# A planned tie between GpSimd and VectorE at their shared port

## The chip, the cores and the metric
The kernel runs on one core of one Trainium2 chip. The metric is the time of one execution in device microseconds; the kernel before takes 1047.97 us as the median of three runs (1047.88, 1047.97 and 1050.83 us). Five engines work side by side, each with its own queue: TensorE (PE), ScalarE (ACT), VectorE (DVE), GpSimd (POOL) and SyncE (SP), which issues the DMAs.

## The reference
Attention with a cut-off is followed by two feed-forward layers on all 2304 tokens:

```
scores = (q @ k.T) / 8                      # batch 4, 8 heads, 576 x 576, head size 64
thresh = max(scores) - tau                  # per row, tau = 0.02
scores = where(scores >= thresh, scores, -1e9)
attn   = exp(scores - max) / (sum + 1e-9)
x      = (attn @ v), heads side by side     # 2304 x 512
h = x @ w_in;   x = (h * clip(h + 3, 0, 6) / 6) @ w_out          # 512 -> 2048 -> 512
h = x @ w2_in;  out = (h / (1 + exp(-1.702 h))) @ w2_out         # 512 -> 2048 -> 512
```

## The kernel before, in words
Products are made at more than half precision by splitting each operand into a high part and a low part (the rest after rounding): three matmuls (high x high, high x low, low x high) stand for one. The high part is written by a ScalarE copy or a VectorE cast; the low part is a subtraction, by VectorE or GpSimd (`tt`, L523, which all such element-wise operations of two tensors share). The split parts of activations are `xh`/`xl` and `g`/`gl`, of keys and queries `kqv`, of weights `inhring`/`inlring` and `outhring`/`outlring`. Weights arrive as 64-bit numbers and are decoded into floats by a chain on ScalarE, VectorE (L575, L576, L577) and GpSimd (`wmstg<-wmstg,wrstg`).

In the first 400 us attention runs head pair by head pair: TensorE makes a 128x576 tile of scores, VectorE takes the row maximum (L837), ScalarE the exponential (L840), VectorE masks and sums (L841), GpSimd or ScalarE multiplies by the reciprocal sum (L856, L864). Half of the first layer is worked in between (L1061, L1086), on 256 or 320 tokens at a time. Then come the second half of the first layer, from 400 to 650 us, and the second layer (L1295, L1431), which uses seven products where eight would be plain, with extra sums and differences `c`, `u`, `p` on VectorE and GpSimd.

Nothing of the order is left to a scheduler. A class `Plan` collects every operation with its engine, an assumed cost and what it reads and writes. `order` plays the plan through as a list schedule: each engine takes its ready operation with the smallest rank (the ranks are stored in the file), and writes a planned start for each operation to `self.start`. For the operations named in `PORT` it keeps VectorE and GpSimd apart: one of them isn't started while one of the other engine runs, by the planned times.

```
PORT = {DVE: {"W", "WH", "WD", "XHB", ...}, POOL: {"kl", "qs", "ql", "vl", "W", "WD", "GD", "N", ...}}
if port[o] and taken[DVE + POOL - e] > t:
    est[o] = taken[DVE + POOL - e]
```

`settle` sorts all operations by planned start, and `fill` turns them into a list of functions that are called in this order, with some matmuls on constants (L1622) put into planned gaps of TensorE. On the chip each engine works off its own operations in this order, and waits for another engine only where a tile's data or its buffer demand it. The planned times themselves are not enforced. `LAT` holds assumed latencies from one engine to another; from VectorE to GpSimd it is 155 ns. The names of operations in the plan (`W` weights, `GL` low part of a gated activation, `XL` low part of an input, `N` normalisation, `RM` spread of reciprocals, `GT` gate on VectorE) are what `PORT` refers to.

Of the kernel before, what the change touches and what calls it, by code (L numbers as in the profile page):

```python
# [3 lines left out]

# [17 lines left out]
PE, ACT, DVE, POOL, SP, DMA = range(6)  # L22

LAT = {
    (PE, PE): 0, (PE, ACT): 197, (PE, DVE): 197, (ACT, PE): 200, (ACT, ACT): 200, (ACT, DVE): 150, (ACT, POOL): 170,
    (DVE, PE): 200, (DVE, ACT): 120, (DVE, DVE): 127, (DVE, POOL): 155, (POOL, PE): 203, (POOL, ACT): 200, (POOL, DVE): 220, (POOL, POOL): 130,
    (SP, DMA): 53, (ACT, DMA): 53, (DMA, PE): 943, (DMA, ACT): 943, (DMA, DVE): 943, (DMA, POOL): 1000, (DMA, SP): 943,
}
# [148 lines left out]
class Plan:  # L177
# [189 lines left out]

    def fill(self, order, make):

        used = [[] for _ in range(BANKS)]  # L370
        for b in self.banks:
            ops = [x[0] for x in b.access]
            used[b.bank].append((min(self.start[o.n] for o in ops), max(self.start[o.n] + o.cost for o in ops) + 250))
        out, end = [], 0.0
        for op in order:
            if op.eng == PE:
                t, s = end, self.start[op.n]
                end = max(end, s + op.cost)
                count = int((s - t) / 450 if s < 12000 else (s - t - 300) / 216)
                if count > 0:  # L380
                    slack = max((min([t - y for _, y in u if y <= t] + [1e9]), -i) for i, u in enumerate(used) if not any(x < s and y > t for x, y in u)) if any(not any(x < s and y > t for x, y in u) for u in used) else None
                    if slack is not None:
                        out.append(make(-slack[1], count))
            out.append(op.fn)
        return out


# [1 line left out]
def tile_top_attention_moe_moe2(  # L389
# [64 lines left out]
    pl = Plan()  # L454
    changed = []

    def add(eng, cost, time, name, fn, rd=(), wr=(), touch=(), alt=None):
        op = pl.add(eng, cost, time, fn, rd, wr, name, touch)
        op.alt = alt
        for c, names in changed:  # L460
            if any(b.pool in names for b in op.bufs):
                op.deps.add(c)
        return op

    def move(time, name, nbytes, fn, rd=(), wr=(), eng=SP):

        op = add(eng, 590, time, name, fn, rd, wr)
        add(DMA, nbytes / 360 * PACE.get(name, 1.0), time, name, lambda: None, rd, wr).deps.add(op)
# [24 lines left out]
    def mark():  # L493
        return Buf(pl, "mark", 1 << 30, None, "")
# [169 lines left out]
    def keep(kept, time):  # L664

        def put(n, reg, src, lo, size):
            d, m = kept.setdefault(n, (dram.tile([P, DM], F32, name="kept"), mark()))
            move(time, "KS", 4 * P * size, lambda: nc.sync.dma_start(out=d[:, reg * HALF:reg * HALF + size], in_=src.t[:, lo:lo + size]), [src], [(m, reg)])

        return put  # L670
# [930 lines left out]
    for q in range(2):  # L1601
        for c0, n in [x for y in ([BLOCKS[1:2], BLOCKS[:1], BLOCKS[2:]], [BLOCKS[1:], BLOCKS[:1]])[q] for x in y]:
            moe2(c0, n, w, t, q == 0, q == 1)
            if left:
                i, kind = left.pop(0)
# [8 lines left out]

    add(ACT, 1500, t, "TL", lambda: nc.scalar.activation(out=gate_b.t, in_=half_b.t, func=ACTF.Gelu_apprx_sigmoid), [half_b], [gate_b]).deps |= {o for o in pl.ops if o.name == "X"}

    def busy(i, count):

        def run():
            t = pools["pm"].tile([P, 512], F32, tag=f"pm{i}", name="pm")  # L1620
            for _ in range(count):
                nc.tensor.matmul(t[:, :P], two_b.t, two_b.t, start=True, stop=True)  # L1622

        return run

    order = pl.settle()
    with tc.manual_schedule():
        for fn in pl.fill(order, busy):
            fn()
# [51 lines left out]
```

## Time and profile before

| | |
|---|---|
| median of 3 runs | 1047.97 us (1047.88 to 1050.83) |
| profiled execution | 1051.93 us, span 1050.1 us |
| TensorE clock, granted share | 0.997 |
| busy: TensorE, VectorE, ScalarE, GpSimd | 98%, 79%, 64%, 55% of the span |

The span runs from the first to the last instruction; the profiled execution's own time holds also what lies around it. A row of a group of instructions gives line, engine, operation, what it writes and reads, shape and count, then busy time and mean duration, then the engine's idle time ahead of them and who ended it. In a timeline an entry in brackets is the idle time of the engine ahead of the instruction, and what ended it.

### The profile page before, as it was taken

To read this page: it belongs to the slowest core of one execution; us is meant where nothing else is said; L and a number is where in the kernel's file an instruction comes from. 1 tells how busy PE (TensorE), PEld (TensorE's weight loads), DVE (VectorE), ACT (ScalarE), POOL (GpSimd) and SP (SyncE) were. 2 spreads that over 40 slices of the span, in tenths; PEclk is the share of its full clock that TensorE was granted. 3 is DMA by queue.
4 is the path that set the end of the run, shared out by engine and by line. 5 is a ranking of instruction groups with operands and counts; after the bars stand their busy time and mean duration, and the time that the engine had idled before them with its cause. 6 is when DMAs were issued, how large, how long until landed. Compare 5 with 4: busy or idle time off the path is not lost. (4 is left out here: it accounts for less than half of the span.)

```text
span 1050.1 us, 21245 instructions
## 1 busy us (share of the span) xinstructions
PE 1028.7 (98%) x7560; PEld 956.4 (91%) x7560; DVE 828.6 (79%) x1700; ACT 667.0 (64%) x1395; POOL 577.0 (55%) x681
## 2 busy tenths in 40 slices
PE   8999999999999999999999999999999999999998
PEld 6787887798979898999899999999999999999998
DVE  7999999998999885768877687756787998656644
ACT  5988678776766665665344444576757766655553
POOL 5577866675656552665564435445654435546452
PEclk9999999999999999999999999999999999999999
DMA  7434466676877665445645768827464896443412
GB/s 237 119 123 125 132 180 181 177 221 165 236 221 190 192 195 150 143 134 179 199 127 178 246 218 268 310 97 255 140 209 156 269 296 193 155 161 104 140 49 72
DMA packets 113194, 187.46 MB, mean 179 GB/s; under 512 B 10816, under 2 KB 62656, under 8 KB 111040
## 3 DMA queue, kind: packets, MB, share of 16 engines
q1 hardware_dynamic: 112944, 185.80, 57.4%
q8 instruction: 60, 0.98, 0.4%
q14 instruction: 46, 0.38, 0.1%
q10 hardware_dynamic: 144, 0.29, 0.1%
HBM read 117.77 MB, written 68.29 MB: 177 GB/s over the span
## 5 line engine op out<-in xcount | busy, mean ns | idle before, releaser
L837 DVE TENSOR_REDUCE nm<-ps 128x1 f32<-128x576 f32 x144 | 105.9, 749 | 14.3 <-PE ps L781 10.5
L523 POOL TENSOR_TENSOR g<-t,g 128x256 fp32r<-128x256 f32 (+2 forms) x84 | 76.1, 909 | 68.9 <-ACT g L520 53.3
L840 ACT ACTIVATE e<-ps,nm 128x576 f32<-128x576 f32 x128 | 93.0, 738 | 31.7 <-DVE nm L837 28.9
L1086 PE MATMUL pm<-g,outhring 128*128 128x256 f32 (+1 forms) x512 | 106.2, 299 | 0.7 <-DVE g L523 0.5
L841 DVE SCALAR_TENSOR_TENSOR e<-ps,th,e 128x576 f32<-128x576 f32 x128 | 102.0, 810 | 6.1 <-ACT e L840 3.0
L1086 PE MATMUL py<-g,outhring 128*128 128x432 f32 (+2 forms) x384 | 99.6, 344 | 2.7 <-DVE yc L523 2.1
L520 ACT ACTIVATE g<-t 128x256 fp32r<-128x256 f32 (+3 forms) x177 | 86.0, 489 | 24.7 <-DVE t L1073 11.3
L523 POOL TENSOR_TENSOR wmstg<-wmstg,wrstg 128x512 uint32<-128x512 uint32 x40 | 55.5, 1390 | 82.2 <-DVE wmstg L577 39.7
L1061 PE MATMUL pm<-xh,inhring 128*128 128x256 f32 (+1 forms) x320 | 97.8, 306 | 0.9 <-DVE t L1073 0.7
L1061 PE MATMUL pm<-xh,inlring 128*128 128x256 f32 (+1 forms) x320 | 94.6, 296 | 0.0
L1061 PE MATMUL pm<-xl,inhring 128*128 128x256 f32 (+1 forms) x320 | 94.5, 295 | 0.0
L781 PE MATMUL ps<-kqv 128*128 128x288 f32 x480 | 82.2, 303 | 3.2 <-DVE e L841 1.9
L1086 PEld LDWEIGHTS pm<-g,outhring 128*128 128x128 f32 x512 | 82.1, 189 | 1.9 <-DVE g L523 0.8
L781 PEld LDWEIGHTS ps<-kqv 128*128 128x128 f32 x480 | 68.1, 190 | 11.0 <-issue 4.5
L1086 PE MATMUL pm<-g,outlring 128*128 128x256 f32 (+1 forms) x256 | 75.7, 296 | 0.0
L1086 PEld LDWEIGHTS py<-g,outhring 128*128 128x128 f32 x384 | 69.9, 191 | 6.2 <-DVE yc L523 2.5
L1086 PE MATMUL py<-g,outlring 128*128 128x432 f32 (+2 forms) x192 | 65.5, 341 | 0.0
L1061 PEld LDWEIGHTS pm<-xh,inhring 128*128 128x128 f32 x320 | 60.6, 189 | 2.5 <-DVE t L1073 0.9
L523 DVE TENSOR_TENSOR g<-t,g 128x256 fp32r<-128x256 f32 (+2 forms) x76 | 49.3, 650 | 16.3 <-ACT g L520 16.0
L1061 PEld LDWEIGHTS pm<-xl,inhring 128*128 128x128 f32 x320 | 60.6, 189 | 0.0
L523 POOL TENSOR_TENSOR kqv<-qk,kqv 64x576 fp32r<-64x576 f32 (+1 forms) x39 | 56.3, 1443 | 7.6 <-DVE kqv L757 3.2
L1061 PEld LDWEIGHTS pm<-xh,inlring 128*128 128x128 f32 x320 | 60.4, 189 | 0.0
(265 smaller groups left out, 3655.2 us busy)
## 6 DMA issues: line engine op xcount, KB each, us to landing
turned<-tr SPq DMA_DIRECT2D x16, 1024.0 KB, 4.1
et<-turned SPq DMA_DIRECT2D x64, 256.0 KB, 5.9
wrawstg<-in_w1i_dram SPq DMA_DIRECT2D x16, 512.0 KB, 3.9
wrawstg<-in_w1o_dram SPq DMA_DIRECT2D x16, 512.0 KB, 3.7
wrawstg<-in_w2i_dram SPq DMA_DIRECT2D x16, 512.0 KB, 4.2
wrawstg<-in_w2o_dram SPq DMA_DIRECT2D x16, 512.0 KB, 4.1
qk<-in_k_dram SPq DMA_DIRECT2D x24, 288.0 KB, 3.9
qk<-in_q_dram SPq DMA_DIRECT2D x24, 288.0 KB, 4.1
```

Of the source, the lines that this page charges most:

```text
L520: return lambda: nc.scalar.activation(out=o(), in_=i(), func=ACTF.Copy, **kw)
L523: return lambda: (nc.vector if eng == DVE else nc.gpsimd).tensor_tensor(out=o(), in0=a(), in1=b(), op=op)
L781: nc.tensor.matmul(ps.t[:, i, :SH], q, w[hd].t[:, i * SH:(i + 1) * SH], start=a, stop=z)
L837: add(DVE, 672, K("R", s), "R", lambda: nc.vector.tensor_reduce(out=nm.t[:, c], in_=ps.t[:, :, :SH], op=ALU.max, axis=AX.XY, negate=True), ...
L840: add(ACT, 624, K("X", s), "X", lambda: nc.scalar.activation(out=ev(), in_=ps.t[:, :, :SH], func=ACTF.Exp, bias=nm.t[:, c]), [ps, (nm, s)] ...
L841: add(DVE, 736, K("M", s), "M", lambda: nc.vector.scalar_tensor_tensor(out=ev(), in0=ps.t[:, :, :SH], scalar=th.t[:, c], in1=ev(), op0=ALU ...
L1061: nc.tensor.matmul(ph.t[:, :n], a, v, start=(cc == 0 and i == 0), stop=(cc == KC - 1 and i == 2))
L1086: nc.tensor.matmul(py.t[:, :n], a, v, start=(st and i == 0), stop=(sp and i == 2))
```

## The change
While the functions are listed, `fill` now keeps what each VectorE operation's function returns, the instruction, under the operation's number. For each GpSimd operation named in `PORT` it looks for the latest VectorE operation (named in `PORT` or not) whose planned end plus 155 ns is no later than the planned start of the GpSimd operation, half a nanosecond allowed, and adds a synchronising dependency of the one's instruction on the other's. If a function returned nothing, the next earlier VectorE operation is taken, and a GpSimd operation whose own function returns nothing gets no dependency. The order of the functions stays.

```diff
     def fill(self, order, make):
+        made, dve = {}, [o for o in order if o.eng == DVE]
+        ends = [self.start[o.n] + o.cost + LAT[DVE, POOL] for o in dve]
+
+        def keep(op):
+            return lambda: made.__setitem__(op.n, op.fn())
+
+        def behind(op, i):
+            return lambda: self.tie(op.fn(), next((made[o.n] for o in dve[i::-1] if made[o.n] is not None), None))
...
-            out.append(op.fn)
+            i = bisect_right(ends, self.start[op.n] + 0.5) - 1 if op.eng == POOL and self.port[op.n] else -1
+            out.append(keep(op) if op.eng == DVE else behind(op, i) if i >= 0 else op.fn)
         return out
...
+    def tie(ins, first):
+        if ins is not None and first is not None:
+            tc.add_manual_dep(ins.ins, first.ins.name, mybir.DependencyInfo(mybir.DependencyClass.Sync, mybir.DependencyReason.ANTI), reason="port")
+
+    pl.tie = tie
```

## Rows read from the trace of the kernel before

**Rows 1.** The page's first part: busy us, share of the span, instructions.

```profile
PE 1028.7 (98%) x7560; PEld 956.4 (91%) x7560; DVE 828.6 (79%) x1700; ACT 667.0 (64%) x1395; POOL 577.0 (55%) x681
```

**Rows 2.** Busy us of each engine (and instructions) in five stretches of the span.

```profile
0.00:200.00 200.00, 191.26 (x1364) 157.00 (x1364) 184.59 (x446) 154.76 (x301) 136.37 (x200) 1.00 0.55 160
200.00:400.00 200.00, 198.36 (x1524) 176.34 (x1525) 180.89 (x432) 138.00 (x289) 120.36 (x194) 1.00 0.71 199
400.00:650.00 250.00, 246.51 (x1504) 235.80 (x1503) 187.63 (x339) 126.99 (x238) 124.73 (x102) 0.99 0.59 182
650.00:1000.00 350.00, 347.17 (x2794) 342.06 (x2793) 255.25 (x451) 223.42 (x509) 176.55 (x168) 1.00 0.57 192
1000.00:1050.10 50.10, 45.42 (x381) 45.22 (x379) 20.24 (x36) 23.86 (x60) 19.00 (x18) 0.98 0.17 53
```

**Rows 3.** Waits of TensorE by releaser: us in total, times, longest us.

```profile
PE py L1086 <- DVE yc L523: 2.1, 2, 1.5
...
PE pm L907 <- DVE pk L856: 0.2, 1, 0.2
```

**Rows 4.** VectorE's instructions by shape: busy us, mean ns, idle before and its releasers.

```profile
L523 DVE TENSOR_TENSOR gl<-c,g 128x512 fp32r<-128x512 f32 x39 | 31.8, 818 | 8.8 <-ACT g L520 4.0 <-ACT t L1374 2.3 <-PE pm L1431 1.3
...
L523 DVE TENSOR_TENSOR g<-t,g 128x256 fp32r<-128x256 f32 x41 | 22.1, 539 | 11.6 <-ACT g L520 11.5
...
L523 DVE TENSOR_TENSOR yc<-py,yc 128x512 f32<-128x512 f32 x28 | 19.1, 686 | 5.2 <-PE py L1431 3.4 <-POOL yc L523 1.5
...
L523 DVE TENSOR_TENSOR c<-pm,p 128x256 f32<-128x256 f32 x40 | 16.8, 419 | 11.5 <-ACT p L520 4.7 <-PE pm L1295 3.9 <-ACT g L520 2.5
...
L523 DVE TENSOR_TENSOR c<-c,p 128x256 f32<-128x256 f32 x15 | 12.3, 821 | 0.4 <-POOL u L523 0.3
```

**Rows 5.** Timeline of all engines, 498 to 510 us: start, us, instruction, idle before.

```profile
498.28 0.69 DVE L577 SCALAR_TENSOR_TENSOR wmstg<-wrawstg,wmstg 128x512 uint32<-128x512 uint32 x1
...
499.11 1.35 POOL L523 TENSOR_TENSOR wmstg<-wmstg,wrstg 128x512 uint32<-128x512 uint32 x1 [1.83 <-DVE wmstg L577]
...
501.43 0.49 DVE L1073 SCALAR_TENSOR_TENSOR t<-t,pm 128x320 f32<-128x320 f32 x1
...
502.03 1.47 POOL L523 TENSOR_TENSOR inlring<-wsstg,inhring 128x512 fp32r<-128x512 f32 x1
...
502.45 1.40 DVE L523 TENSOR_TENSOR g<-t,g 128x320 fp32r<-128x320 f32 x1
...
503.44 1.55 POOL L523 TENSOR_TENSOR inlring<-wmstg,inhring 128x512 fp32r<-128x512 f32 x1
...
503.78 1.50 DVE L523 TENSOR_TENSOR wmstg<-wmstg,wsstg 128x256 f32<-128x256 f32 x1
...
506.07 0.56 PE L1086 MATMUL py<-g,outhring 128*128 128x320 f32 x2 [0.52 <-DVE yc L523]
...
508.76 0.80 PE L1086 MATMUL py<-g,outhring 128*128 128x256 f32 x2 [1.55 <-DVE yc L523]
```

**Rows 6.** Timeline of all engines, 80 to 87 us.

```profile
81.13 1.46 POOL L523 TENSOR_TENSOR outlring<-wmstg,outhring 128x512 fp32r<-128x512 f32 x1
81.37 1.36 DVE L1074 CAST g<-t 128x256 fp32r<-128x256 f32 x1
...
86.23 0.97 PE L821 MATMUL ps<-kqv 128*128 128x288 f32 x3 [0.87 <-PE pm L983]
```

**Rows 7.** Timeline of all engines, 486 to 492 us.

```profile
487.47 0.29 PE L1061 MATMUL pm<-xh,inlring 128*128 128x256 f32 x1
...
487.59 0.28 PE L1061 MATMUL pm<-xh,inhring 128*128 128x256 f32 x1
...
489.79 1.29 POOL L523 TENSOR_TENSOR wmstg<-wmstg,wrstg 128x512 uint32<-128x512 uint32 x1 [3.95 <-DVE wmstg L577]
489.91 1.45 DVE L523 TENSOR_TENSOR g<-t,g 128x256 fp32r<-128x256 f32 x1 [0.26 <-ACT g L520]
...
491.42 0.38 PE L1086 MATMUL py<-g,outhring 128*128 128x256 f32 x1 [0.62 <-DVE g L523]
```

More of the change, by code (lines that the diff above doesn't have):

```diff
@@ L1 @@
 from base64 import b85decode
+from bisect import bisect_right
 from contextlib import ExitStack
```

## Prediction, made before the result
> **What bounds the kernel now.** I read the engines' shares first [rows 1]. TensorE is busy for 1028.7 us of a span of 1050.1 us, so at most 21.4 us can go without touching its matmuls. VectorE is at 79% and GpSimd at 55%. The reader is to see that the target is not an engine's work but TensorE's idle time, and that GpSimd has 473 us in which it could wait.
>
> Then the same by stage [rows 2]. TensorE idles 8.7 us in the first 200 us, 1.6, 3.5 and 2.8 us in the three stages that follow, and 4.7 us in the last 50 us, where the last matmul is over and results drain. In the first 400 us VectorE is busy for 365 us of 400: there a microsecond that VectorE loses reaches TensorE soon. After 400 us it has a quarter to a third of its time free, and a lost microsecond matters only where TensorE is already waiting.
>
> Then TensorE's waits by releaser [rows 3]. Without the first matmul's wait for a constant, 17 rows name VectorE, from "py <- yc" at 2.1 us to "pm <- pk" at 0.2 us, 23 waits and 11.9 us in all. None names GpSimd. So GpSimd does not hold TensorE up directly; if it does harm, it does so through VectorE.
>
> That it does is seen in the mean of one VectorE operation by shape [rows 4]. A 128x256 subtraction or addition with one input in PSUM takes 419 ns. The same operation with both inputs in SBUF has a mean of 821 ns (c<-c,p) and 539 ns (g<-t,g). At 128x512 it is 686 ns with PSUM and 818 ns (gl<-c,g) without. These three shapes alone lose (821-419)x15 + (539-419)x41 + (818-686)x39 = 6.0 + 4.9 + 5.1 = 16 us; other shapes whose operands are all in SBUF are stretched in the same way, the ones with PSUM are not.
>
> The timeline shows how [rows 5]. At 502.03 us GpSimd starts a subtraction of 1.47 us. At 502.45 VectorE starts g<-t,g (128x320) and is done only at 503.85, after GpSimd; the same work behind a free port takes 0.49 us (VectorE's t<-t,pm of that size in [rows 5]). At 503.44 GpSimd has started its next subtraction, and VectorE's operation at 503.78, a 128x256 addition that takes 0.42 us behind a free port [rows 4], takes 1.50 us. VectorE is now (1.40 - 0.49) + (1.50 - 0.42) = 2.0 us late, and TensorE idles 0.52 us at 506.07 and 1.55 us at 508.76, both times for VectorE's yc. A port that one engine holds for its whole operation delays the other, one for one, and the delay arrives at TensorE.
>
> **The change part by part.** It adds to each GpSimd operation named in PORT, except the RM multiplications (their function returns nothing, so nothing can be tied), one wait on a VectorE operation. From 681 GpSimd instructions [rows 1] go 46 memsets, one addition for the second identity and the 20 RM operations: about 614 ties. It removes and reorders nothing, and adds no work to VectorE, ScalarE, TensorE or SP.
>
> The partner is the last VectorE operation, whatever its kind, whose planned end plus 155 ns is not after the planned start. I took the partners from the planned starts that the kernel before computes. Where the plan was kept, the partner is long done, and the wait costs nothing but its issue. Where GpSimd runs ahead of the plan, it now stands back until VectorE has caught up.
>
> The gain, case by case. Both GpSimd operations of [rows 5] run ahead. The partner of the one at 502.03 is the very g<-t,g that it blocks, and that of the one at 503.44 lies five operations behind the one that it blocks. With the ties both VectorE operations keep their short time, VectorE is 2.0 us earlier, and the 2.07 us of idle time go. In [rows 6] the GpSimd operation at 81.13 is tied to a t<-t,pm three operations behind the cast at 81.37, which takes 1.36 us, as it cannot end before GpSimd; TensorE's wait at 86.23 (0.87 us, named after its own matmul, because VectorE's late reduction and masking free the PSUM tile at the last moment) goes. Five more cases have this shape, with GpSimd operations at 19.20, 109.39, 175.88, 707.31 and 852.40 us and TensorE idle for 0.37, 0.92, 0.54, 0.53 and 0.35 us behind them. Sum: 2.07 + 0.87 + 2.71 = 5.65 us in eight waits.
>
> Two corrections. The end of a matmul is modelled: in [rows 7] one takes 0.29 us while the next starts 0.12 us after it, so each idle stretch is shown about 0.17 us too short; eight of them make 1.4 us, sum 7.0 us. And idle below the threshold of the view, and waits of VectorE's own followers on ScalarE, are not in the list; as VectorE's stretch in the three shapes above is 16 us and the cases above recover some 8 us of stretch in all, I add 3 us, an estimate bounded below by 0 and above by the other 6.3 us of the 11.9 us that VectorE releases. Sum: 10 us.
>
> The cost. A GpSimd operation that has to wait starts some 0.14 us after the VectorE operation's end: 498.28 + 0.69 = 498.97, and GpSimd starts at 499.11 [rows 5]. If all 614 waited, that were 86 us of GpSimd's 473 us of idle time; if none waits it is zero, and a wait that is already met adds at most an instruction of the sequencer. I take zero for the end of the kernel, because no row of [rows 3] has TensorE waiting for GpSimd. The cover is that slack, stage by stage: 63.6 us in the first 200 us, over 170 us from 650 to 1000 [rows 2].
>
> What is queued behind a waiting operation: GpSimd's own next ones, in order. The subtraction at 503.44 would stand back some 3 us, until its partner has run, and the g<-t,g of GpSimd behind it starts about 1 us later. Its result feeds the second product of an output group that comes three gates later, several microseconds on; the decoded weights are used over 100 us later. The buffers that these operations free are taken by ScalarE's next decode, which is not near TensorE either. SP's queue sees later stores only through GpSimd's few results that are stored.
>
> What is late next: where the partner lies ahead of the VectorE operation that is blocked, and is already done, nothing is protected. That is so for GpSimd at 489.79 us [rows 7], whose partner was done, while VectorE's g<-t,g waits for ScalarE until 489.91 and is then blocked (TensorE idle 0.62 us). Such cases stay. By the partners I expect about half of VectorE's stretch to stay.
>
> A rule of the Trainium skill weighs against the change. In [rows 4] c<-pm,p has its 419 ns although GpSimd is busy in more than half the time. SBUF — State Buffer, "Who interferes with whom", says that a VectorE instruction with at most one SBUF input, outside the two-port modes, does not contend with GpSimd, and the row agrees. By it a tie to a reduction or masking that reads PSUM protects no port and only holds GpSimd up; what that could cost is the third rival. By the cases above the sum stays a gain of 10 us.
>
> **The sum.** The profiled execution took 1051.93 us; less 10 us it is 1041.9. That execution lies 3.96 us above the median of the three runs, 1047.97 us, like the slowest of the three. For the median I take off the same 10 us: 1038 us.
>
> **The rivals.** First, more is gained: all 23 waits that VectorE ends go, 11.9 + 23 x 0.17 = 15.8 us, and some of the idle below the threshold, 2 us: 1030 us. For it: in the first 400 us VectorE is nearly full, and there a late start carries over from one head to the next. Against it: half the collisions are not covered.
>
> Second, nothing comes of it: GpSimd, held to the plan on one side only, collides with the next VectorE operation in place of this one; a VectorE operation that waits for ScalarE finds the port taken, as in [rows 7]. The exchange leaves VectorE's stretch where it is: 1047 to 1049 us. That the ties don't work at all (an operation's function that returns nothing) would look the same; only for RM does the code show it.
>
> Third, slower: in the first 200 us GpSimd becomes the bound. There it has 63.6 us free, and about 160 tied operations among its 200. A VectorE operation takes 184.59/446 = 0.41 us there; if each tie costs half of one and the 0.14 us, that is 160 x 0.35 = 56 us, and GpSimd is nearly full. It then delivers kl, ql and the scaled rows late, TensorE's scores wait for it, and a tenth of the 56 us that reaches TensorE makes 5.6 us: 1054 us. It decides once less than some 10 us of GpSimd's idle time are left in this stage. For it: the ties do not ask what the partner reads. Against it: most partners are done when GpSimd starts.
>
> **How the numbers follow.** The forecast has a chance of 0.50, more gain 0.26, nothing 0.14, slower 0.10. The forecast's own range is 1033 to 1044 us, by 4 us for what is not recovered and 5 us for what is not listed. Two in ten are left out at 1027 below and 1048 above. A run of this kernel can be told from no change at 0.3%, 3.1 us, so faster is below 1044.8 us: 0.50 + 0.26 and a little of the second case, 0.78; same 0.12; slower 0.10.
>
> **What would show it.** Right: the three shapes of [rows 4] fall towards 419 and 686 ns while c<-pm,p stays; VectorE's busy time falls by 20 us or more at the same count; the stretched pairs of [rows 5, 6] are gone, with GpSimd starting behind its partner; GpSimd's waits on VectorE grow by tens of microseconds; TensorE's waits on yc, gl and e shrink. Wrong: TensorE waiting for GpSimd's results (kqv, g, xl), GpSimd over 90% in the first 200 us, or VectorE's means unchanged. If VectorE's busy time falls and the end does not move, the lost time was hidden, and the step from VectorE to TensorE is the one that failed.

## Result and profile after

The changed kernel takes 1037.29 us (median; 1035.86 to 1037.47), the kernel before, timed beside it, 1048.48 us (1047.88 to 1050.83). The ratio is 0.9886, 95% interval 0.9868 to 0.9904: 11 to 12 us faster. The forecast was 1038 us, a gain of 10 us. The profiled execution took 1037.47 us, span 1035.7 us; the one before took 1051.93 us, which is 3.5 us above the median of its runs, so the two profiles lie 14.5 us apart and hold some 3 us more than the medians do. Line L523 and those up to the end of the products' code stand 11 lines lower (L534 for L523), the matmuls on constants 17 (L1639 for L1622).

The page's first part (busy us, share, instructions), which answers to [rows 1]:

```profile
PE 1023.2 (99%) x7560; PEld 954.6 (92%) x7560; DVE 792.7 (77%) x1700; ACT 667.2 (64%) x1395; POOL 566.0 (55%) x681
```

At the same counts VectorE's busy time fell by 35.9 us and GpSimd's by 11.0 us. ScalarE's is as before (667.2 against 667.0 us). Busy time by stage, which answers to [rows 2]; the columns are the stretch, its length, then TensorE, weight loads, VectorE, ScalarE and GpSimd, and the granted clock:

```profile
0.00:200.00 200.00, 194.38 (x1390) 159.87 (x1392) 183.89 (x458) 158.08 (x307) 136.11 (x204) 1.00 0.57 164
200.00:400.00 200.00, 199.38 (x1542) 177.26 (x1539) 178.12 (x421) 135.97 (x285) 117.07 (x191) 1.00 0.71 197
400.00:650.00 250.00, 248.86 (x1513) 239.60 (x1510) 181.12 (x347) 130.48 (x244) 129.18 (x107) 1.00 0.62 190
650.00:1000.00 350.00, 349.31 (x2864) 346.79 (x2863) 235.12 (x453) 226.82 (x518) 170.57 (x169) 1.00 0.56 188
```

TensorE's idle time is now 5.6, 0.6, 1.1 and 0.7 us in these stages (8.7, 1.6, 3.5 and 2.8 us in [rows 2]). With the last stretch it is 12.5 us against 21.4. That is 8.9 of the 14.4 us by which the two spans differ; the other 5.5 us are in TensorE's busy time, at the same counts. GpSimd is as busy in the first 200 us as it was, 68%.

TensorE's waits by releaser (us in total, times, longest), which answers to [rows 3]:

```profile
PE pm L1639 <- DVE two L552: 1.4, 1, 1.4
PE py L1097 <- POOL g L534: 1.0, 1, 1.0
PE ps L792 <- DVE e L852: 0.9, 3, 0.3
...
PE ps L792 <- DVE rc L859: 0.2, 1, 0.2
```

Without the wait for the constant `two`, VectorE now releases 10 waits and 3.8 us, against 23 and 11.9. All waits for `yc`, `gl`, `c` and `p` are gone. The second row is new: TensorE waits for GpSimd.

VectorE by shape (busy us, mean ns), which answers to [rows 4]:

```profile
L534 DVE TENSOR_TENSOR gl<-c,g 128x512 fp32r<-128x512 f32 x39 | 28.3, 729 | 8.8 <-ACT g L531 3.7 <-ACT t L1385 2.5 <-PE pm L1442 1.3
...
L534 DVE TENSOR_TENSOR yc<-py,yc 128x512 f32<-128x512 f32 x28 | 19.2, 688 | 8.5 <-PE py L1442 5.5 <-POOL yc L534 1.5 <-ACT outhring L531 1.2
...
L534 DVE TENSOR_TENSOR g<-t,g 128x256 fp32r<-128x256 f32 x41 | 18.9, 461 | 11.4 <-ACT g L531 11.1
...
L534 DVE TENSOR_TENSOR c<-pm,p 128x256 f32<-128x256 f32 x40 | 16.8, 421 | 13.2 <-PE pm L1306 5.8 <-ACT p L531 4.7 <-ACT g L531 2.5
...
L534 DVE TENSOR_TENSOR c<-c,p 128x256 f32<-128x256 f32 x15 | 8.7, 577 | 0.4 <-POOL u L534 0.3
```

The three shapes with both inputs in SBUF fell (818 to 729, 539 to 461, 821 to 577 ns); the two with an input in PSUM stay at 688 and 421 ns.

The stretch of [rows 5] begins here at 494.7 us. Timeline of VectorE (start, us, instruction):

```profile
494.68 0.48 DVE L534 TENSOR_TENSOR g<-t,g 128x320 fp32r<-128x320 f32 x1
495.08 0.42 DVE L534 TENSOR_TENSOR wmstg<-wmstg,wsstg 128x256 f32<-128x256 f32 x1
...
497.10 1.11 DVE L534 TENSOR_TENSOR xl<-xr,xh 128x432 fp32r<-128x432 f32 x2
```

and of GpSimd, with the idle time ahead and its releaser in brackets:

```profile
495.24 1.41 POOL L534 TENSOR_TENSOR inlring<-wsstg,inhring 128x512 fp32r<-128x512 f32 x1 [0.77 <-DVE g L534]
497.84 1.52 POOL L534 TENSOR_TENSOR inlring<-wmstg,inhring 128x512 fp32r<-128x512 f32 x1 [1.20 <-DVE xl L534]
```

g<-t,g takes 0.48 us (1.40 before) and the addition 0.42 us (1.50 before). The first GpSimd subtraction waits for g<-t,g, the second for the low part `xl`, 2.3 us after the addition that it used to block. The cast of [rows 6] takes 0.29 us (1.36 before), and TensorE has no idle time between 80 and 87 us:

```profile
80.38 0.29 DVE L1085 CAST g<-t 128x256 fp32r<-128x256 f32 x1
```

The case of [rows 7] has gone too. VectorE's g<-t,g came 0.12 us behind GpSimd's decode step before; now it comes 0.03 us ahead of it and takes 0.42 us (timeline of all engines, 482 to 485 us):

```profile
483.40 0.42 DVE L534 TENSOR_TENSOR g<-t,g 128x256 fp32r<-128x256 f32 x1
483.43 1.55 POOL L534 TENSOR_TENSOR wmstg<-wmstg,wrstg 128x512 uint32<-128x512 uint32 x1 [3.31 <-ACT g L531]
```

TensorE's 0.62 us at this place are gone. With nine ties only (run one below) the collision is still there and TensorE waits 0.9 us.

What is left and what is new. GpSimd's next decode step blocked VectorE's L575 before (timeline, 495.9 to 497 us):

```profile
496.00 1.28 POOL L523 TENSOR_TENSOR wmstg<-wmstg,wrstg 128x512 uint32<-128x512 uint32 x1 [0.63 <-DVE wmstg L577]
496.18 1.39 DVE L575 TENSOR_SCALAR wmstg<-wmstg 128x512 f32<-128x512 f32 x1
```

In the change the same GpSimd operation blocks the operation after that one (timeline of all engines, 488 to 493 us):

```profile
488.79 1.40 POOL L534 TENSOR_TENSOR wmstg<-wmstg,wrstg 128x512 uint32<-128x512 uint32 x1 [0.35 <-DVE yc L534]
...
489.07 1.39 DVE L587 TENSOR_SCALAR wmstg<-wmstg 128x512 uint32<-128x512 uint32 x1
```

GpSimd waits for its partner `yc`, and the next VectorE operation at the port, a decode step with a mean of 470 ns, takes 1.39 us. This collision has stayed and only moved by one operation; TensorE has no idle time near it. And the new wait (timeline of all engines, 512 to 518 us):

```profile
513.64 1.30 POOL L534 TENSOR_TENSOR wmstg<-wmstg,wrstg 128x512 uint32<-128x512 uint32 x1 [1.88 <-DVE t L1199]
...
513.96 1.26 DVE L586 TENSOR_SCALAR wmstg<-wmstg 128x512 f32<-128x512 f32 x1 [0.41 <-ACT wmstg L585]
...
515.14 0.48 DVE L534 TENSOR_TENSOR yc<-py,yc 128x320 f32<-128x320 f32 x1
...
515.77 1.14 POOL L534 TENSOR_TENSOR g<-t,g 128x432 fp32r<-128x432 f32 x1 [0.83 <-DVE yc L534]
...
516.97 0.46 PE L1097 MATMUL py<-g,outhring 128*128 128x432 f32 x1 [1.03 <-POOL g L534]
```

GpSimd stands idle for 0.83 us for a tie to `yc`, starts 0.15 us after `yc` ends, and TensorE waits 1.03 us for its result. What makes `yc` late is GpSimd's own operation before: at 513.64 its partner was done, VectorE's L586 waited for ScalarE until 513.96 and was then blocked (1.26 us, mean 559 ns), and `yc` stands behind it.

### The profile page after: what moved, and what is told of

Read it like the earlier page. It is cut to its first block, busy times and chain, and to the rows that moved or that the text cites. A ratio compares the mean times of both kernels' runs of the same rounds, so it can differ in the third digit from the quotient of the medians.

```text
span 1035.7 us, 21355 instructions
## 1 busy us (share of the span) xinstructions
PE 1023.2 (99%) x7560; PEld 954.6 (92%) x7560; DVE 792.7 (77%) x1700; ACT 667.2 (64%) x1395; POOL 566.0 (55%) x681
## 4 chain that ended last, share of the span: by engine, by line
PE 78%; DVE 8%; DMA 6%; POOL 3%; ACT 2%; issue 2%; SPq 1%; POOLq 0%; DVEq 0%; ACTq 0%
PE pm L1306 18%; PE py L1442 11%; PE py L1097 8%; PE pm L1072 7%; PE pm L1097 7%; PE pm L1187 6%; PE pm L1442 6%; PE ps L792 4%; PE pm L1010 4%; PE pm L918 2%; DVE e L852 2%; DVE nm L848 2%; DMA qk<-in_q_dram 1%; DMA wrawstg<-in_w2i_dram 1%; DMA wrawstg<-in_w1i_dram 1%
## 5 line engine op out<-in xcount | busy, mean ns | idle before, releaser
L534 POOL TENSOR_TENSOR g<-t,g 128x256 fp32r<-128x256 f32 (+2 forms) x84 | 74.1, 884 | 67.0 <-ACT g L531 16.6
L534 POOL TENSOR_TENSOR wmstg<-wmstg,wrstg 128x512 uint32<-128x512 uint32 x40 | 55.1, 1377 | 74.7 <-DVE wmstg L588 31.1
L534 POOL TENSOR_TENSOR kqv<-qk,kqv 64x576 fp32r<-64x576 f32 (+1 forms) x39 | 56.0, 1436 | 9.0 <-DVE g L534 2.5
L1358 ACT ACTIVATE pm<-id 128x256 f32<-128x256 f32 (+1 forms) x98 | 37.2, 385 | 31.1 <-DVE c L534 30.6
```

Of the source, the lines that this page charges most:

```text
L534: return lambda: (nc.vector if eng == DVE else nc.gpsimd).tensor_tensor(out=o(), in0=a(), in1=b(), op=op)
```

## Experiments

A gain is one minus the ratio, times the median of the kernel before in the same set of runs. Some expectations count 634 GpSimd operations with a partner; 20 of them are the RM multiplications that get no tie, so there are 614 ties.

**One. Nine ties.** The eight GpSimd operations of the forecast's sum, and one at 506.59 us that lies between the two waits of [rows 5].

```diff
+SOME = {23, 123, 680, 1596, 3292, 3294, 3832, 4663, 5540}
-i = bisect_right(ends, self.start[op.n] + 0.5) - 1 if op.eng == POOL and self.port[op.n] else -1
+i = bisect_right(ends, self.start[op.n] + 0.5) - 1 if op.n in SOME else -1
```

> Only the nine GpSimd operations of the eight cases that the forecast added up keep their tie (19.20, 81.13, 109.39, 175.88, 502.03, 503.44, 506.59, 707.31 and 852.40 us in the run before); the other 605 have none. Port theory, by the forecast's sum: 7 us of the 11 us come, 1041 to 1042 us beside 1048.5 before. If a recovered stall is eaten by the next one: 1044 to 1047. Rival, that the gain is GpSimd's general pace, in proportion to the number of ties: 9/614 of 11 us, so 1048.

Measured: 1039.96 us, ratio 0.9923 (0.9911 to 0.9936), a gain of 8.1 us, some 1 us more than the 1041 to 1042 us expected. The page's first part:

```profile
PE 1025.2 (99%) x7560; PEld 955.0 (92%) x7560; DVE 823.2 (79%) x1700; ACT 666.1 (64%) x1395; POOL 575.3 (55%) x681
```

VectorE's busy time fell by only 5.4 us. Nine ties out of 614 bring two thirds of the gain with a seventh of VectorE's saving.

**Two and three. The ties split in two.** In the trace of before 114 of the tied GpSimd operations start while the partner is still running or has yet to run; for the other 500 it is done. One kernel ties the 114 alone, one the 500 alone.

```diff
+SOME = {23, 33, 93, 121, 123, ...}
-... if op.eng == POOL and self.port[op.n] else -1
+... if op.n in SOME else -1                                             # the 114
+... if op.eng == POOL and self.port[op.n] and op.n not in SOME else -1  # the 500
```

> Ties only on the 114 GpSimd operations that in the run before started while their partner was still running. Port theory: these are the only ties that move anything, so the whole gain comes, 1036 to 1038.5 us. Rival, pace: 114/614 of 11 us, 1046. Rival, that ties on the others protect a changed schedule: 1039 to 1042.

> The complement: ties on the other 500 GpSimd operations alone, whose partner had ended when they started. Port theory: each wait is met when it comes, and its issue is hidden in GpSimd's idle time: 1047.5 to 1049 us, no change. Rival, pace: 500/614 of 11 us, 1039. Rival, that 500 more waits cost GpSimd time that matters: 1050 or more.

Measured: the 114 alone 1037.57 us, ratio 0.9893 (0.9877 to 0.9909), the whole gain; VectorE's busy time is 793.2 us, as with all ties. The 500 alone 1046.69 us, ratio 0.9984 (0.9974 to 0.9993), 1.7 us. VectorE's busy time is 830.6 us there, not less than before. The theory's 1047.5 to 1049 us was missed by 0.8 us: the interval leaves out 1, so the 1.7 us (0.7 to 2.8) are small but probably real. GpSimd's listed waits on VectorE are 226.5 us there against 191.0 before, so by the profile some of the 500 ties are waited for.

**Four. Every partner one VectorE operation earlier.**

```diff
-i = bisect_right(ends, self.start[op.n] + 0.5) - 1 if ...
+i = bisect_right(ends, self.start[op.n] + 0.5) - 2 if ...
```

> All ties, each to the VectorE operation one earlier than in the change. Port theory: the partner is now mostly one ahead of the operation that would be blocked, so GpSimd comes in front of it again; VectorE's busy time returns to 820 us or more and 7 to 9 of the 11 us are lost: 1044 to 1047 us. Rival, pace: GpSimd is held nearly as well, 1037 to 1040.

Measured: 1045.59 us, ratio 0.998 (0.9968 to 0.9991), a gain of 2.1 us; VectorE 827.4 us. It has the same number of waits, and most of the gain is gone: what pays is which operation is waited for.

**Five and six. Ties in one half of the kernel only.**

```diff
-... if op.eng == POOL and self.port[op.n] else -1
+... if op.eng == POOL and self.port[op.n] and self.start[op.n] < 386000 else -1    # early
+... if op.eng == POOL and self.port[op.n] and self.start[op.n] >= 386000 else -1   # late
```

> Ties only on GpSimd operations that are planned to start in the first 386 us (attention, about 400 us on the chip). If the gain is spread over the stages as TensorE's idle time fell between the two traces (8.7 to 5.6 us in the first 200 us, 1.6 to 0.6 us in the next 200, of 8.9 us in all, and the gain of 11.2 us in that proportion), this kernel keeps about 5 us: 1042 to 1045 us. Rival, that VectorE is so full in attention that a late start carries over there from head to head and nearly all of the gain comes from it: 1037 to 1040 us. Rival, that attention's ties cost as much as they give, since many of their partners read PSUM and GpSimd has least free time there: 1047 us or more.

> The other ties alone, on GpSimd operations planned to start after 386 us. By the fall of TensorE's idle time in those stages (3.5 to 1.1, 2.8 to 0.7, 4.7 to 4.5 us) about 6 us of the gain: 1041 to 1044 us, and the two halves add up to the whole gain within 2 us. Rival of the full VectorE in attention: 1046 to 1049 us. Rival of ties in attention that cost: 1035 us or less, under the changed kernel.

Measured: early 1043.78 us, ratio 0.9952 (0.9936 to 0.9969), 5.0 us; late 1039.88 us, ratio 0.9922 (0.99 to 0.9944), 8.2 us, 1.1 us more than expected. They add up to 13.2 us against 12.0 us for the whole, within the 2 us allowed. The full VectorE of attention is not what makes the gain.

**Seven. Partners only among VectorE operations named in PORT.** 347 of the 614 ties get another partner; most of the partners given up read PSUM.

```diff
-made, dve = {}, [o for o in order if o.eng == DVE]
+made, dve = {}, [o for o in order if o.eng == DVE and self.port[o.n]]
```

> The partner is the latest VectorE operation that is itself named in PORT, so that no GpSimd operation waits for a reduction, masking or addition that reads PSUM and does not touch the port for long. Theory: such partners cost nothing, because GpSimd's wait is covered by its idle time, and they give something, because they hold GpSimd to the plan: as the changed kernel or a little worse, 1036 to 1040 us. Rival, that ties behind operations with a PSUM input only hold GpSimd up: faster than the changed kernel, 1034 us or less.

Measured: 1036.14 us, ratio 0.9884 (0.9863 to 0.9905), as the change. Ties behind operations that are not named in PORT, most of which read PSUM, cost nothing that can be measured. The Trainium skill (SBUF — State Buffer, "Who interferes with whom") says that a VectorE operation with at most one input in SBUF, outside the two-port modes, does not contend with GpSimd; the 421 and 688 ns above agree. Whether the tie goes to such an operation or to the PORT operation ahead of it makes no difference to the end here.

**Eight. No allowance for the hand-over.** The partner may end at the planned start; 283 of the 614 ties get a later partner, 198 of them one that is planned to end exactly then.

```diff
-ends = [self.start[o.n] + o.cost + LAT[DVE, POOL] for o in dve]
+ends = [self.start[o.n] + o.cost for o in dve]
```

> The partner may end at the planned start of the GpSimd operation, without the 155 ns that the change allows for the hand-over; so a number of GpSimd operations get a partner one VectorE operation later. Theory: the operations that were blocked were mostly one to several behind the partner's place in the plan, and the few that lie within 155 ns of the edge change little: 1035 to 1039 us. Rival, that the collisions which stay are those that the 155 ns leave open: 1031 to 1034 us. Rival, that the later partner holds GpSimd up so that its own results come late: 1040 us or more, with TensorE waiting for GpSimd in more places than one.

Measured: 1042.96 us, ratio 0.9951 (0.9932 to 0.997), a gain of 5.1 us; by the medians 5.7 us slower than the change. The theory's range was missed and its premise was wrong: almost half of the partners change, not a few. The third reading is what the trace shows. TensorE's longest waits besides the one for the constant:

```profile
PE py L1097 <- POOL g L534: 2.5, 3, 2.0
...
PE ps L792 <- DVE e L852: 1.2, 5, 0.3
```

and the timeline of all engines that leads to the longest:

```profile
517.41 0.49 DVE L534 TENSOR_TENSOR yc<-py,yc 128x320 f32<-128x320 f32 x1
...
517.46 1.29 POOL L534 TENSOR_TENSOR wmstg<-wmstg,wrstg 128x512 uint32<-128x512 uint32 x1 [2.12 <-DVE wmstg L586]
...
517.82 1.22 DVE L587 TENSOR_SCALAR wmstg<-wmstg 128x512 uint32<-128x512 uint32 x1
...
519.21 1.51 POOL L534 TENSOR_TENSOR g<-t,g 128x432 fp32r<-128x432 f32 x1 [0.45 <-DVE wmstg L587]
...
520.77 0.47 PE L1097 MATMUL py<-g,outhring 128*128 128x432 f32 x1 [2.03 <-POOL g L534]
```

GpSimd starts at 517.46, behind its partner (L586), and blocks VectorE's L587 (1.22 us, mean 500 ns in this run). Its next operation, the g<-t,g that TensorE needs, is tied to that same L587: GpSimd waits for the operation that it has itself just held up, as it does in the change at 515.77 by way of `yc`. TensorE's waits for GpSimd are 1.5 us longer than in the change; the rest of the 5.7 us is not traced. VectorE's busy time is 809.0 us here, 16 us more than with the change, so later partners protect less and not more.

**Nine. Both sides keep the plan.** As eight, and each VectorE operation named in PORT also waits for the latest such GpSimd operation that is planned to end ahead of it.

```diff
+pool = [o for o in order if o.eng == POOL and self.port[o.n]]
+pends = [self.start[o.n] + o.cost for o in pool]
...
+j = bisect_right(pends, self.start[op.n] + 0.5) - 1 if self.port[op.n] else -1
...
+    self.tie(made[op.n], next((made[o.n] for o in pool[j::-1] if made[o.n] is not None), None))
```

> Both sides keep the plan: each GpSimd operation named in PORT waits for the latest VectorE operation planned to end ahead of it, and each VectorE operation named in PORT waits likewise for the latest such GpSimd operation, both without the 155 ns. Theory: a wait is free only on the engine with idle time. VectorE's stretch goes almost whole (g<-t,g 128x256 at about 420 ns, c<-c,p likewise, VectorE's busy time at 740 to 760 us), but VectorE, which is 77 to 92% busy by stage, now waits for GpSimd in its queue, with everything behind it: slower than the kernel before, 1052 to 1066 us. Rival, that the stretch itself is the cost and its whole removal pays more: 1028 to 1034 us, faster than the change.

Measured: 1065.12 us, ratio 1.0162 (1.014 to 1.0184), 17 us slower than before. The page's first part, and three of VectorE's shapes (L548 is L534 of the change):

```profile
PE 1036.7 (98%) x7560; PEld 955.6 (90%) x7560; DVE 748.2 (70%) x1700; ACT 670.7 (63%) x1395; POOL 535.7 (50%) x681
```

```profile
L548 DVE TENSOR_TENSOR gl<-c,g 128x512 fp32r<-128x512 f32 x39 | 26.7, 687 | 11.7 <-POOL gl L548 6.2 <-ACT t L1399 1.9 <-POOL c L548 1.3
...
L548 DVE TENSOR_TENSOR g<-t,g 128x256 fp32r<-128x256 f32 x41 | 17.2, 421 | 16.9 <-POOL c L548 6.5 <-ACT g L545 4.2 <-POOL gl L548 2.5
...
L548 DVE TENSOR_TENSOR c<-c,p 128x256 f32<-128x256 f32 x15 | 6.3, 422 | 4.9 <-POOL c L548 2.0 <-POOL yc L548 1.4 <-POOL gl L548 0.8
```

All three shapes have the length of their twins that read PSUM (688 and 421 ns above), so 748.2 us is about VectorE's work without stretch: some 80.4 us of its 828.6 us in [rows 1] were stretch, and the change took out 35.9, 45%. With next to no stretch left the kernel is slowest, 22 us slower than run eight, whose ties it shares. VectorE waits instead: its listed waits on GpSimd grow from 16.2 us before to 189.4 us. TensorE's idle time is 26.5 us (21.4 before); its busy time is 8.0 us longer, which is not traced. VectorE's largest waits on GpSimd are

```profile
DVE c L548 <- POOL g L548: 12.7, 7, 2.9
DVE wmstg L600 <- POOL wmstg L548: 11.4, 13, 2.3
DVE gl L548 <- POOL gl L548: 10.8, 7, 3.9
```

**Ten to twelve. The allowance at 40, 310 and 600 ns.** 78, 154 and 367 of the 614 ties get another partner than in the change.

```diff
-ends = [self.start[o.n] + o.cost + LAT[DVE, POOL] for o in dve]
+ends = [self.start[o.n] + o.cost + 40 for o in dve]    # or 310, or 600
```

> 40 ns in place of the 155 ns. 81 of the ties then have a later partner than in the change, against 293 without any allowance; the 204 whose later partner is planned to end just when the GpSimd operation starts keep the partner of the change. Theory: what cost 5 us without the allowance is these 204, where the wait is always met last, GpSimd starts a hand-over late and VectorE's next operation is already at the port: 1036 to 1039 us, as the change. Rival, that every partner inside the hand-over costs alike, or those 40 to 155 ns away cost most: 1040 us or more, with TensorE waiting for GpSimd's g for over 2 us.

> 310 ns in place of the 155 ns: 158 of the ties have an earlier partner than in the change, against all of them in the kernel with partners one operation earlier, which kept 2.4 us of the gain. Theory: a partner that is one operation too early leaves the operation behind it unprotected, so a part of the gain goes: 1038 to 1043 us, VectorE's busy time between 793 and 827 us. Rival, that the ties need only hold GpSimd loosely to the plan: as the change, 1036 to 1038 us.

> 600 ns in place of the 155 ns: 377 of 634 partners lie earlier than in the change, among them those of 76 of the 114 GpSimd operations that started while their partner ran, and of six of the nine that were tied alone; at 310 ns it was 22 of the 114 and two of the nine, and nothing was lost. Theory: the gain goes with the partners of these few operations, whatever the rest do: most of it is lost, 1042 to 1046 us, VectorE's busy time above 815 us. Rival, that holding GpSimd loosely to the plan is enough, and one operation earlier for every tie was only too loose: as the change or faster, 1034 to 1038 us.

Measured: 1036.91 us, ratio 0.9891 (0.9874 to 0.9907); 1035.33 us, ratio 0.9875 (0.986 to 0.989); 1040.48 us, ratio 0.9925 (0.9909 to 0.9941). At 40 ns the theory held: what costs 5.7 us in eight are the 205 ties that differ there and that 40 ns leave as in the change, 190 of them with a partner in eight that is planned to end just as GpSimd starts. At 310 ns the theory fell: nothing is lost, VectorE stays at 792.8 us, and the kernel has the lowest median of all, below the rival's 1036 to 1038 us, though its interval overlaps that of the change. At 600 ns most should have gone, and 7.9 us stayed (VectorE 812.6 us), between the two theories.

Single places follow the theory even where the sums do not. TensorE's idle time ahead of the scores behind the GpSimd operations at 175.88 and 109.39 us was 0.69 and 0.92 us in the trace of before; with the change these waits are 0.28 and 0.31 us. The first operation loses its partner at 310 ns, the second only at 600 ns. At 310 ns (timeline of TensorE):

```profile
109.02 1.82 PE L792 MATMUL ps<-kqv 128*128 128x288 f32 x12 [0.23 <-DVE e L852]
...
175.59 0.79 PE L792 MATMUL ps<-kqv 128*128 128x288 f32 x4 [0.81 <-DVE e L852]
```

and at 600 ns:

```profile
111.75 1.43 PE L792 MATMUL ps<-kqv 128*128 128x288 f32 x9 [0.90 <-DVE e L852]
```

Each wait is back in the run in which its partner moved. What the looser ties at 310 ns give in return is not shown. No row there has TensorE waiting for GpSimd, so the 1.03 us of the change are not spent; but neither has run two such a row, and it takes as long as the change.

## Why the prediction was right

- **The bound and the mechanism.** Right. TensorE's work is unchanged and its idle time fell from 21.4 to 12.5 us. Of the 5.5 us by which its busy time fell some 1.4 us are the clock (next point), and 13 waits for VectorE fewer, each shown some 0.17 us too short by the prediction's reading, would make 2.2; the rest is not traced. The three shapes fell and the two controls with PSUM stayed. Run four shows that it is the partner that counts, and not the waits as such.
- **The eight cases, 7.0 us with the correction for modelled ends.** Right in place, and in size within the noise: nine ties gave 8.1 us (6.7 to 9.3). What the profile shows beside it is TensorE's clock. Within the 1.55 us of idle time of [rows 5] the granted clock of the profiled execution of before fell to the half level, as a view by stretches shows (TensorE's busy us behind the length, the clock is the third number from the right):

```profile
508.00:508.50 0.50, 0.00 (x0) 0.00 (x0) 0.50 (x2) 0.00 (x0) 0.00 (x0) 0.82 0.78 104
508.50:511.50 3.00, 2.74 (x12) 2.74 (x13) 3.00 (x10) 0.69 (x1) 0.00 (x0) 0.50 0.75 228
511.50:512.00 0.50, 0.50 (x5) 0.50 (x5) 0.50 (x3) 0.00 (x0) 0.00 (x0) 0.76 0.01 2
512.00:514.00 2.00, 2.00 (x16) 2.00 (x16) 1.65 (x4) 0.00 (x0) 0.62 (x1) 1.00 0.70 193
```

  At 0.50, which is 1.2 GHz, 12 matmuls start in 3 us; at 1.00, 2.4 GHz, 16 in 2 us. Half of the 2.74 us of work, some 1.4 us, is lost to the clock. In the traces of the change and of the nine ties the clock stays up from 486 to 530 us. This bears on the distance between the two profiles and hardly on that of the medians. The two traces that show such a fall have a mean clock of 0.997 and 0.998, and all others 0.999 or 1.000. Of 51 further executions of the kernel before, timed beside the experiments, 9 have 0.998 or less, with a median of 1049.8 us; the other 42 have a median of 1047.9 us.
- **The 3 us that were only estimated.** Right in size, within wide intervals: the whole gain of 12.0 us (10.1 to 13.8) less 8.1 us leaves some 4 us. Most of it comes from the rest of the 114 operations (run two), and it is poor: VectorE saves another 30.5 us for it. Most of VectorE's saving does not reach the end. The upper bound given for this term, 6.3 us, was too low: the waits at 23.97 and 86.23 us in the sum have TensorE's own matmuls as releaser, so they are not among the 11.9 us, and 7.5 us of those were left.
- **About half of the stretch stays.** Right: 55% by run nine. The form that was named (the partner done, VectorE waiting for ScalarE and then blocked) is seen at 513.96 us. It went, though, in the very place for which it was forecast: the collision of [rows 7] and TensorE's 0.62 us there are gone, as VectorE comes first by 0.03 us. Which of the other ties brings that is not traced.
- **A cost of zero.** Not quite, and one of the prediction's own signs of being wrong appeared. TensorE waits 1.03 us for a GpSimd result that a tie held back, behind a `yc` that GpSimd itself had made late. The cover was argued from [rows 3], where no row names GpSimd; a wait that isn't there yet has no row. Otherwise the cover held: GpSimd's listed waits on VectorE grew from 191 to 299 us, but all its listed waits together went from 457.5 to 454.6 us. The ties replaced waits that would have come anyway, above all those for ScalarE's data (184 us before, 89 us with the change), and GpSimd's own operations became shorter.
- **The rivals.** Nothing (1047 to 1049 us) is refuted by the time and by VectorE's means; its mechanism, a collision with the next operation instead, is seen at 489.07 us. More gain (1030 us) did not come, though 8.1 of the 11.9 us that VectorE released went. Slower through a full GpSimd: it is busy for 136.11 us of the first 200, against 136.37 us. Its mechanism, GpSimd's results coming late, is real all the same: the change shows it once, and run eight, with partners no more than 155 ns later in the plan, loses 5.7 us with it in view.

Open: why 500 ties whose partner was done in the trace of before still give 1.7 us; and why so much is left at 600 ns, where six of the nine ties, and 76 of the 114, have lost their partner, while one operation earlier for all leaves only 2.1 us.

## What to carry to other kernels

When two engines share a port, look for the places where the bound engine waits behind a blocked operation, and tie those: nine waits did two thirds of the work of 614. Let the engine with idle time do the waiting: with VectorE waiting as well, the stretch was gone and the kernel 17 us slower than before. Leave some time for the hand-over in the choice of what to wait for (40 ns were enough here, none was not), or the waiting engine arrives late, blocks the next operation and then waits for it. Busy time saved on an engine that is not the bound is no measure of the gain: 5.4 us of it brought 8 us, and the next 30 brought about 4.

## Hardware behaviour that was not expected

- A blocked VectorE operation holds up the very engine that blocks it: in run eight GpSimd's 1.29 us operation stretches L587 to 1.22 us (mean 0.50), and GpSimd's next one, tied to L587, starts 0.46 us after its own predecessor has ended (518.75 to 519.21).
- In the profile of before the granted clock fell to half within an idle stretch of 1.55 us on TensorE and stayed there for 3.4 us, and likewise in that of the early ties alone at one of 1.54 us. In that of the 500 other ties, with the same idle time of 1.54 us at the same place, it did not fall, nor in that of run eight at 2.03 us. The same wait can thus cost some 1.4 us more in one execution than in another.
- `tensor_scalar` with one input in SBUF is blocked as well as the operations with two: L587 takes 1.39 us in place of a mean of 470 ns. The Trainium skill's section cited above (SBUF — State Buffer, "Who interferes with whom") has that for the two-port modes of such an operation; the row agrees that it is blocked, and no row shows the mode. The forecast had it only in general, among the other shapes whose operands are all in SBUF.
